# An mLSTM cell with a SwiGLU layer behind it: VectorE's weighing, a scaling step, two loads and a few clears change places

## The chip, the cores and the metric

One core of one Trainium2 chip runs the whole program. The metric is the device time of one execution in microseconds, as the median of several runs. The profile of a run is that of one execution.

## The reference

```python
def _attn_ref(q, k, v, i_gate, f_gate, o_gate):      # q, k, v, o_gate: (4, 8, 768, 40); gates: (4, 8, 768)
    ...                                              # C, n start at 0, m at -1e30
    for t in range(S):
        kt, vt, qt = (k[:, :, t], v[:, :, t], q[:, :, t])
        m_new = np.maximum(f_gate[:, :, t] + m, i_gate[:, :, t])
        f_stab = np.exp(f_gate[:, :, t] + m - m_new)
        i_stab = np.exp(i_gate[:, :, t] - m_new)
        m = m_new
        C = f_stab[:, :, None, None] * C + i_stab[:, :, None, None] * np.einsum('bhd,bhe->bhde', vt, kt)
        n = f_stab[:, :, None] * n + i_stab[:, :, None] * kt
        h_tilde = np.einsum('bhde,bhe->bhd', C, qt)
        nq = np.einsum('bhd,bhd->bh', n, qt)[:, :, None]
        denom = np.maximum(np.abs(nq), 1.0)
        o = 1.0 / (1.0 + np.exp(-o_gate[:, :, t]))
        y[:, :, t] = o * h_tilde / denom
    return y

def _moe_ref(x, w_gate, w_val, w_out):               # x: (3072, 320), weights: (320, 1536) twice, (1536, 320)
    g = x @ w_gate
    silu = g * (1.0 / (1.0 + np.exp(-g)))
    val = x @ w_val
    return silu * val @ w_out
```

The cell's output, with its heads side by side, is the input x of the layer. The three weight matrices come as float64, the rest as float32.

## The kernel before

**Tiling.** The 768 tokens of the sequence are cut into six groups of 128. Group 0 is attended in one piece (128 tokens at once), the later ones in halves of 64 with a state C carried between them. The 32 pairs of batch and head are worked in two parts P of 16. For each group of 4 x 128 tokens the layer then computes 12 blocks of 128 hidden features (`NFC`), and their product with `w_out`.

**Order.** The order on every engine is the order of the program's text: there is no planner, each engine has one queue, and an instruction that waits holds back all behind it. DMAs are issued from SP's queue, some from GpSimd's (the value halves of the weights). Two pools of PSUM banks, "cell" and "gen", have four banks each and hand them out in turn.

**The head (0 to 27 us of the profile).** SP issues the loads of q, k, v and the output gate for group 0, then the first weights. VectorE, GpSimd and ScalarE clear paddings and build masks; PE computes group 0's decay weights as sums in PSUM (`first_mask` L569, `first_inputs` L573, `first_maxima` L578), ScalarE exponentiates them, PE transposes q and k (`turn_one`, L352, which reads the padded columns too), computes scores (`first_scores`), the output rows (`first_own`), their transposes (`seam`, L508) and the first state (`first_state` L640, two banks of "gen"). `first_kept` (L643) copies that state to SBUF on ScalarE. `spread` copies the densely loaded q and k into tiles of 64 columns a head of which 40 are filled; `q_sb` and `k_sb` have their 24 columns of padding cleared. `keep1` is a row of ones with a zero at the head of every 64, needed by `late_sums`. `late_gates` (L156) loads the gates of groups 1 to 5, 80 KB each, which `late_sums` reads in the hidden layer of group 0.

**The weights.** They arrive as pairs of 32-bit words in pieces (`piece_load`: a gate half from SP's queue and a value half in two parts from GpSimd's). Pieces 0 to 3 hold one block each, pieces 4 to 7 two. Pieces 2 and 3 land in a part of `h_sb`, and their loads wait for a small memset there (L693, L701). A block is converted to float32 in three steps (`convert`): `scale` on ScalarE (two instructions, L226 into `top` and L228 into `low`; `top` has one buffer, `low` two), `join` on VectorE (L235, L236) and `rounded` (L243), on GpSimd by default and on VectorE where `on_vector` or the call says so. Block 0 is done in two portions (L253, L254). Silu's function table is loaded ahead of time by a one-element activation on `warm` (L715).

`fill("add", 12, False)` (L557) issues 12 matmuls on zeros into a spare part of a bank, whose result nobody reads.

**Group 0's hidden layer (27 to 88 us).** The loop at L1060 calls `hidden(0, m, ...)` for the 12 blocks: 20 matmuls into two banks of "gen" (L759), then the steps handed over as `first` (conversions of later blocks), then Silu on ScalarE (L764) and the product on VectorE (L765). Behind each block the steps of `slots[m]` follow: the attention of group 1 is spread over them. `do_scores` puts group 1's scores into all four banks of "cell"; `do_weigh` (`weigh`, L392) multiplies them with the decay weights on VectorE; `do_add` takes banks of "cell" again; `do_intra` reads the weighed scores.

```python
for m in range(NFC):
    first = [run(convert, j, V if j in on_vector else None) for j in ahead[m]]
    first += {10: [run(scale, 12), run(join, 12)], 11: [run(convert, 13)]}.get(m, [])
    hidden(0, m, first, amid.get(m, ()))
    for f in slots.get(m, ()):
        f()
```

Groups 1 to 5 follow with fewer products a block (`gated` L929, `project_seven` L830, L835). The change does not touch them.

Of the kernel before, what the change touches and what calls it, by code (L numbers as in the profile page):

```python
# [24 lines left out]
def kernel(  # L25
# [18 lines left out]
    nc = tc.nc  # L44
    B, H, S, D = q.shape
# [28 lines left out]
    def flat(t):  # L74
        return t.rearrange("p c t -> p (c t)")
# [22 lines left out]
    def half(i):  # L98
        return slice(i * SUB, (i + 1) * SUB)
# [5 lines left out]
    def heads(P):  # L105
        return slice(P * UH, (P + 1) * UH)

    k_sb = const.tile([128, BH, DP], F32)
    q_sb = const.tile([128, BH, DP], F32)
    v_sb = const.tile([128, BH, D1], F32)  # L110
    o_sb = const.tile([128, BH, D], F32)
# [19 lines left out]
    f_sb, i_sb, keep1 = (x_flat[0:BH, ds(5 * L + n * (NS - 2) * SUB, (NS - 2) * SUB)].rearrange("p (s t) -> p s t", t=SUB)  # L131
                         for n in range(3))
# [8 lines left out]
    def copy(eng, dst, src):  # L141
        if eng is nc.scalar:
            nc.scalar.copy(dst, src)
        else:
            eng.tensor_copy(dst, src)

    def gate_rows(a):
        return a.rearrange("b h s -> (b h) s")
# [7 lines left out]
    def late_gates():  # L156
        nc.sync.dma_start(out=flat(f_sb), in_=gate_rows(f_gate)[:, L:])
        nc.sync.dma_start(out=flat(i_sb), in_=gate_rows(i_gate)[:, L:])
# [7 lines left out]
    def piece_load(p, home=None, parts=(0, 1, 2)):  # L166
        kind, m, n = PIECES[p]
        if kind == "gv":
            a, d = NKC, n * 128
            gate_w, val_w = (w[:, m * 128:(m + n) * 128].rearrange("(c p) f -> p c f", p=HP) for w in (moe_w_gate, moe_w_val))  # L170
            src = [(slice(0, HP), slice(0, NKC), gate_w), (slice(HP, 128), slice(0, NKC - 1), val_w[:, 1:]),
                   (slice(HP, 128), slice(NKC - 1, NKC), val_w[:, 0:1])]
        else:
            a, d = n, DM
            src = [(slice(0, 128), slice(0, n), moe_w_out[m * 128:(m + n) * 128].rearrange("(a p) d -> p a d", p=128))]
        if src[0][2].dtype == F32:
            for r, cs, w in [src[x] for x in parts if x < len(src)]:
                if kind == "o":
                    nc.sync.dma_start(out=wo_sb[r, m:m + n, :], in_=w)
                else:  # L180
                    for x in range(n):
                        nc.sync.dma_start(out=wgv_sb[r, m + x, cs], in_=w[:, :, ts(x, 128)])
            return
        if p in homes:
            raw = homes[p]
        else:
            if p < 4:
                if p == 0:
                    homes["raw"] = conv.tile([128, 4 * NKC * 128], U32, name="raw")
                base = homes["raw"] if p < 2 else raw_h.rearrange("p m t -> p (m t)").bitcast(U32)  # L190
                raw = base[:, ds(2 * (p % 2) * a * d, 2 * a * d)]
            elif home is None:
                raw = conv.tile([128, 4 * NKC * 128], U32, name="raw")
            else:
                raw = home.rearrange("p a t -> p (a t)").bitcast(U32)
            raw = homes[p] = raw[:, 0:2 * a * d]
        for x in parts:
            if x < len(src):
                r, cs, w = src[x]
                eng = nc.gpsimd if x else nc.sync  # L200
                eng.dma_start(out=raw[r].rearrange("p (a d) -> p a d", a=a)[:, cs], in_=w.bitcast(U32))
        words = raw.rearrange("p (a d two) -> p a d two", two=2, a=a)
        raws[p] = (words[:, :, :, 0], words[:, :, :, 1])
        split(p)
# [4 lines left out]
    def split(p):  # L209
        if p in raws:  # L210
            lo, hi = raws.pop(p)
            kind, m, n = PIECES[p]
            if kind == "gv":
                for c in range(n):
                    r = slice(c * 128, (c + 1) * 128)
                    blocks[m + c] = (lo[:, :, r], hi[:, :, r], wgv_sb[:, m + c])
            else:
                for c in range(0, n, 2):
                    blocks[NFC + (m + c) // 2] = (lo[:, c:c + 2], hi[:, c:c + 2], wo_sb[:, m + c:m + c + 2, :])

    def scale(j):
        if j in blocks:
            lo, hi, dst = blocks[j]
            a, d = hi.shape[1], hi.shape[2]
            top = conv.tile([128, NKC * 128], F32, name="top", bufs=1).rearrange("p (a d) -> p a d", a=a)
            nc.scalar.mul(top, hi.bitcast(F32), 2.0 ** -112)  # L226
            low = conv.tile([128, NKC * 128], I32, name="low").rearrange("p (a d) -> p a d", a=a)
            nc.scalar.mul(low, lo, 2.0 ** -29)  # L228
            blocks[j] = (low, top.bitcast(U32), dst)

    def join(j):
        if j in blocks:
            lo, top, dst = blocks[j]
            both = dst.bitcast(U32)
            nc.vector.tensor_scalar(both, top, scalar1=3, scalar2=None, op0=ALU.logical_shift_left)  # L235
            nc.vector.scalar_tensor_tensor(both, in0=top, scalar=0x80000000, in1=both, op0=ALU.bitwise_and,  # L236
                                           op1=ALU.bitwise_or)
            blocks[j] = (lo, dst.bitcast(I32))

    def rounded(j, eng=None):  # L240
        if j in blocks:
            lo, dst = blocks.pop(j)
            (eng or nc.gpsimd).tensor_tensor(dst, dst, lo, op=ALU.add)  # L243
# [13 lines left out]
    def convert(j, eng=None):  # L257
        scale(j)
        join(j)
        rounded(j, eng)  # L260
# [6 lines left out]
    def spread(eng, x, dst, P):  # L267
        copy(eng, dst[:, heads(P), 0:D], dense[:, x])
# [16 lines left out]
    nc.gpsimd.affine_select(mask, mask, compare_op=ALU.is_ge, fill=NEG, base=0, pattern=[[1, L]], channel_multiplier=-1)  # L285
    nc.vector.memset(keep0, 1.0)
    nc.vector.memset(step0, 0.0)
    nc.gpsimd.memset(q_sb[:, :, D:], 0.0)
    nc.gpsimd.memset(v_sb[:, :, D:], 1.0)
    ident_b = early.tile([128, 128], BF16)  # L290
    nc.vector.tensor_copy(ident_b, ident)
# [259 lines left out]
    def fill(name, n, thin):  # L551
        for x in range(n):
            i = x % 2
            if thin:
                nc.tensor.matmul(spare_of[name, 1][half(i)], lhsT=junk[:, 0:SUB], rhs=junk[:, H * D1:], start=True, stop=True)
            else:
                nc.tensor.matmul(spare_of[name, i], lhsT=junk[half(i), 0:128], rhs=junk[half(i), H * D1:], start=True,  # L557
                                 stop=True)
# [4 lines left out]
    A, V, G = nc.scalar, nc.vector, nc.gpsimd  # L563
# [17 lines left out]
    def first_exp(P):  # L581
        for x in range(B):
            h = P * UH + x * HH
            nc.scalar.activation(W0[:, h:h + HH], wps[P, x], AF.Exp)
# [6 lines left out]
    def first_values(P):  # L591
        nc.gpsimd.tensor_tensor(vw_sb[:, heads(P)], v_sb[:, heads(P)], w_end[:, heads(P)].to_broadcast([128, UH, D1]),
                                op=ALU.mult)
# [49 lines left out]
    def first_kept(P, ps, eng):  # L643
        copy(eng, state(2)[:, P * UA:(P + 1) * UA], ps)
# [11 lines left out]
        first_inputs(1, x)  # L656
    spread(V, 0, q_sb, 0)
    spread(G, 1, k_sb, 0)
    nc.vector.memset(k_sb[:, :, D:], 0.0)
    nc.vector.memset(keep1, 1.0)  # L660
    nc.vector.memset(keep1[:, :, 0:1], 0.0)
    first_exp(0)
    turn_one(0, q_sb, qT, (V, A))
    turn_one(0, k_sb, kT, (V, A))
# [16 lines left out]
    turn_one(1, k_sb, kT, (A, A), "gen")  # L681
    nc.scalar.activation(warm, warm, AF.Sigmoid)
    first_values(1)
    late_gates()
    first_x(0)
    first_own(1)
    first_x(1)
# [11 lines left out]
    first_gate(1, (G, V), V)  # L699
    piece_load(2)  # L700
    nc.gpsimd.memset(flat(raw_h)[:, 2 * NKC * 128:2 * NKC * 128 + 1], 0.0)  # L701
    piece_load(3)
    piece_load(4)
    portion(0, slice(0, 2))
# [6 lines left out]
    blocks.pop(0, None)  # L711
    join((0, 2))
    rounded((0, 2), V)
    fill("add", 12, False)
    nc.scalar.activation(warm, warm, AF.Silu)  # L715
    convert(1, V)
    first_kept(0, ps0, A)
    first_kept(1, ps1, A)
    convert(2, V)
# [314 lines left out]
    def load_all(dst, a, n, eng=nc.sync):  # L1034
        for P in range(2):
            load(dst, a, n, P, eng)

    run = lambda f, *a, **b: (lambda: f(*a, **b))


    on_vector = (9, 10, 11)
    ahead = {0: [], 1: [3], 2: [4], 3: [5], 4: [6], 5: [7], 6: [8], 7: [9], 8: [10], 9: [11], 10: [], 11: []}
    slots = {
        0: [run(piece_load, 5), run(piece_load, 6, wo_sb)],
        1: [run(late_sums)],
# [4 lines left out]
        6: [run(piece_load, 7, parts=VALUE)] + [run(turn_one, P, k_sb, kT, (A, A)) for P in range(2)] + [run(weights_cap, 0), run(weights_cap, 1), run(piece_load, 8)],  # L1050
        7: [run(weights_sub, 1, 0), run(weights_sub, 1, 1), run(weights_exp, 0), run(weights_exp, 1), run(weigh_values, G, 0),
            run(weigh_values, G, 1)],
        8: [run(nc.gpsimd.memset, q_sb, 0.0), run(do_scores), run(piece_load, 9), run(load_all, o_sb, o_gate, 1)],
        9: [run(do_weigh, 0), run(do_weigh, 1), run(do_decayed, 2)],
        10: [run(do_add, 1, (0,)), run(rounded, 12), run(load_squares, q_sq, q, 2, (0,))],
        11: [run(do_intra, 0), run(do_inter, 1, 0), run(do_gather, 1, 0, False), run(piece_load, 10),
             run(load_squares, q_sq, q, 2, (1,))],
# [1 line left out]
    amid = {8: [run(turn_one, P, q_sb, qT, (A, A)) for P in range(2)], 11: [run(do_add, 1, (1,)), run(do_state, 2)]}  # L1059
    for m in range(NFC):  # L1060
        first = [run(convert, j, V if j in on_vector else None) for j in ahead[m]]
        first += {10: [run(scale, 12), run(join, 12)], 11: [run(convert, 13)]}.get(m, [])
        hidden(0, m, first, amid.get(m, ()))
        for f in slots.get(m, ()):
            f()
# [115 lines left out]
```

## Time and profile before

| what | value |
|---|---|
| median of 3 runs | 507.34 us (507.01 to 509.08) |
| profiled execution | 507.06 us, span 505.3 us |
| granted TensorE clock | 0.999 |
| PE busy in 0:26.99 | 24.62 us |
| PE busy in 26.99:31.84 | 4.56 us of 4.85 |
| PE busy in 31.84:53.50 | all 21.66 us |
| PE busy in 70:96 | 25.87 us of 26.00 |
| DMA in 26.99:31.84 | 233 GB/s, share of the engines 1.06 |

The span runs from the first to the last instruction on the core; the time of the execution has 1.76 us more around it. Busy time of an engine leaves out instructions that only wait, branch or issue DMAs. The share of DMA can come out above 1, since a packet's time holds its own waiting.

### The profile page before, as it was taken

What the parts mean: (1) busy time and instruction counts of PE and PEld (TensorE: products, weight loads), DVE (VectorE), ACT (ScalarE), POOL (GpSimd) and SP (SyncE); (2) the same over time, 40 slices, a digit from 0 to 9 for tenths busy, and PEclk for the clock granted to TensorE, in tenths of its full rate; (3) what the DMA queues carried; (4) which work ended last, traced back from release to release, by engine and by line L of the source; (5) the groups of instructions that cost most, each with busy time, mean ns of one, the idle gap of its engine ahead of it and who ended that gap; (6) DMA issues with size and microseconds to landing.
All of it is one profiled execution on the core that took longest, in us unless ns stands there. A gap on an engine that the chain in (4) does not pass through costs nothing.

```text
span 505.3 us, 15069 instructions
## 1 busy us (share of the span) xinstructions
PE 499.4 (99%) x6427; PEld 423.6 (84%) x6427; DVE 334.6 (66%) x544; ACT 209.3 (41%) x407; POOL 260.2 (51%) x292
## 2 busy tenths in 40 slices
PE   8999999999999999999999999999999999999997
PEld 3855555767888899988899888899888899988897
DVE  6779767889998687578376677477568554233421
ACT  3775783467262256323248312339321340223210
POOL 3743533458877834466633357643357650166710
PEclk9999999999999999999999999999999999999999
DMA  9999998797706991403992502991101200000001
GB/s 143 188 262 220 170 229 180 155 173 106 104 4 100 161 93 48 54 3 58 165 111 34 87 4 44 165 131 20 42 3 22 34 2 27 27 0 1 1 14 39
DMA packets 184746, 43.29 MB, mean 86 GB/s; under 512 B 173000, under 2 KB 180184, under 8 KB 184040
## 3 DMA queue, kind: packets, MB, share of 16 engines
q1 hardware_dynamic: 183284, 38.26, 47.6%
q0 software_dynamic: 1264, 4.02, 3.1%
q8 instruction: 50, 0.82, 0.7%
q14 instruction: 16, 0.13, 0.1%
q10 hardware_dynamic: 132, 0.07, 0.0%
HBM read 35.68 MB, written 4.01 MB: 79 GB/s over the span
## 4 chain that ended last, share of the span: by engine, by line
PE 92%; SPq 3%; DMA 2%; DVE 2%; issue 1%; ACT 1%; DVEq 0%; ACTq 0%
PE gv_x L929 26%; PE o_ps L830 21%; PE gv_y L929 21%; PE gv_ps L759 9%; PE o_ps L776 5%; PE inter L434 2%; PE sp L385 2%; PE intra L443 2%; SPq L139 2%; DMA raw<-in_moe_w_gate_dram 2%; PE add L411 2%; PE o_ps L835 1%; SPq L265 1%; DVE w_sb L520 0%; DVE wgv_sb L236 0%
## 5 line engine op out<-in xcount | busy, mean ns | idle before, releaser
L929 PE MATMUL gv_x<-xT,wgv_sb 64*128 64x256 f32 x720 | 89.1, 377 | 0.0
L929 PEld LDWEIGHTS gv_x<-xT,wgv_sb 64*128 64x128 f32 x720 | 69.5, 187 | 7.9 <-issue 0.2
L830 PE MATMUL o_ps<-wo_sb,h_sb 128*128 128x160 f32 x456 | 63.9, 300 | 0.0
L830 PEld LDWEIGHTS o_ps<-wo_sb,h_sb 128*128 128x128 f32 x456 | 62.3, 190 | 1.7 <-issue 1.7
L977 ACT ACTIVATE h_sb<-gv_x 128x256 f32<-128x256 f32 x30 | 11.5, 384 | 116.3 <-PE gv_x L929 116.3
L759 PE MATMUL gv_ps<-xT,wgv_sb 64*128 64x512 f32 x240 | 53.6, 595 | 0.6 <-DVE wgv_sb L243 0.6
L759 PEld LDWEIGHTS gv_ps<-xT,wgv_sb 64*128 64x128 f32 x240 | 24.3, 187 | 24.8 <-issue 23.2
L929 PE MATMUL gv_y<-xT,wgv_sb 64*128 64x256 f32 x360 | 43.9, 376 | 0.0
L929 PE MATMUL gv_y<-q_sb,wgv_sb 64*128 64x256 f32 x360 | 43.9, 376 | 0.0
L396 POOL TENSOR_TENSOR vw_sb<-v_sb,w_sb 128x656 f32<-128x656 f32 x10 | 13.6, 1361 | 49.0 <-ACT w_sb L535 38.1
L929 PEld LDWEIGHTS gv_y<-q_sb,wgv_sb 64*128 64x128 f32 x360 | 35.0, 187 | 3.9
L929 PEld LDWEIGHTS gv_y<-xT,wgv_sb 64*128 64x128 f32 x360 | 35.0, 187 | 3.9
L535 ACT ACTIVATE w_sb<-w_sb,g_T 128x64 f32<-128x64 f32 x128 | 31.0, 333 | 0.0
L929 PE MATMUL gv_x<-q_sb,sw 64*128 64x256 f32 x240 | 30.9, 376 | 0.0
L830 PE MATMUL o_ps<-wT,S 128*128 128x160 f32 x216 | 30.2, 299 | 0.0
L830 PEld LDWEIGHTS o_ps<-wT,S 128*128 128x128 f32 x216 | 29.6, 190 | 0.0
L970 POOL TENSOR_TENSOR tmp<-tmp 128x512 f32<-128x512 f32 x15 | 20.0, 1333 | 16.8 <-DVE tmp L969 16.8
L950 POOL TENSOR_TENSOR h_sb<-x_sb 128x512 f32<-128x512 f32 x12 | 15.7, 1305 | 24.6 <-ACT x_sb L949 24.6
L950 POOL TENSOR_TENSOR h_sb<-tmp 128x512 f32<-128x512 f32 x13 | 16.5, 1271 | 21.5 <-ACT tmp L949 21.5
L797 POOL TENSOR_TENSOR S<-h_sb 128x256 f32<-128x256 f32 x30 | 22.6, 755 | 9.2 <-DVE h_sb L950 7.2
L776 PE MATMUL o_ps<-wo_sb,h_sb 128*128 128x320 f32 x96 | 27.4, 439 | 0.0
L969 DVE TENSOR_TENSOR tmp<-tmp,gv_y 128x1024 f32<-128x1024 f32 x15 | 18.1, 1205 | 13.7 <-PE gv_y L929 12.0
(234 smaller groups left out, 1008.2 us busy)
## 6 DMA issues: line engine op xcount, KB each, us to landing
w_sb<-M_dram SPq DMA_DIRECT2D x10, 512.0 KB, 6.7
v_sb<-in_v_dram SPq DMA_DIRECT2D x12, 320.0 KB, 6.2
o_sb<-in_o_gate_dram SPq DMA_DIRECT2D x12, 320.0 KB, 5.8
raw<-in_moe_w_out_dram SPq DMA_DIRECT2D x3, 1280.0 KB, 7.1
k_sb<-in_k_dram SPq DMA_DIRECT2D x10, 320.0 KB, 7.2
x_sq<-k_sb SPq DMA_DIRECT2D x64, 40.0 KB, 3.3
q_sb<-in_q_dram SPq DMA_DIRECT2D x32, 64.0 KB, 3.6
raw<-in_moe_w_gate_dram SPq DMA_DIRECT2D x3, 640.0 KB
```

The source lines that it names most:

```text
L139: eng.dma_start(out=dst[:, heads(P), 0:D], in_=tokens(a, c, P))
L396: eng.tensor_tensor(vw_sb[:, heads(P)], v_sb[:, heads(P)], w_sb[:, heads(P), last].to_broadcast([128, UH, D1]), op=ALU.mult)
L535: nc.scalar.activation(w_sb[:, h], w_sb[:, h], AF.Exp, bias=g_T[:, n, h:h + 1], scale=-1.0)
L759: nc.tensor.matmul(ps[i], lhsT=wgv_sb[half(i), m, kc, :], rhs=x[half(i), kc, :], start=(kc == 0), stop=(kc == NKC - 1))
L776: nc.tensor.matmul(ps[u], lhsT=hid(g, m)[:, ts(u, L)], rhs=wo_sb[:, m, :], start=(m == 0), stop=(m == NFC - 1))
L797: eng.tensor_tensor(S1[:, k], lo[:, second_half], hi[:, second_half], op=ALU.add)
L830: nc.tensor.matmul(node[x][:, i], lhsT=lhs(k)[:, ts(i, L)], rhs=rhs(k), start=start and k == 0 and i == 0, stop=stop and k == KH - 1, skip ...
L929: nc.tensor.matmul(ps[:, i, cols], lhsT=lhs(c)[half(i)], rhs=rhs(c)[half(i)], start=start and c == 0, stop=stop and c == n - 1, skip_group ...
L950: (nc.vector if k == KH - 1 else nc.gpsimd).tensor_tensor(h_sb[:, 2 * k + 1], uw[:, 0], uw[:, 1], op=ALU.mult)
L969: nc.vector.tensor_tensor(uw, uw, y, op=ALU.add)
L970: nc.gpsimd.tensor_tensor(uw[:, :, second_half], uw[:, :, second_half], uw[:, :, first_half], op=ALU.add)
L977: nc.scalar.activation(h[:, first_half], x[:, 0, first_half], AF.Silu)
```

## The change

In the head, `q_sb`'s padding is cleared by VectorE behind its copy of q instead of by GpSimd at the start, and `keep1` is built by GpSimd behind its copy of k instead of by VectorE. The two late gate loads move in SP's queue from ahead of piece 2's gate half to behind it. Six of the 12 matmuls on zeros go. Block 1's two scaling instructions stand ahead of Silu's table load on ScalarE instead of behind it.

In group 0's hidden layer, block 11 is no longer converted in one go behind block 9's matmuls. Its scaling stays there; its join and rounding (still on VectorE) move to the slot behind block 9, thus behind block 9's product. The weighing of group 1's scores moves from the slot behind block 9 into the slot behind block 8, so that on VectorE it stands ahead of block 9's product and block 11's join. ScalarE's order is the same there, as is PE's and GpSimd's.

```diff
@@ -285,7 +285,6 @@
-    nc.gpsimd.memset(q_sb[:, :, D:], 0.0)
@@ -656,9 +655,10 @@
     spread(V, 0, q_sb, 0)
     spread(G, 1, k_sb, 0)
+    nc.vector.memset(q_sb[:, :, D:], 0.0)
     nc.vector.memset(k_sb[:, :, D:], 0.0)
-    nc.vector.memset(keep1, 1.0)
-    nc.vector.memset(keep1[:, :, 0:1], 0.0)
+    nc.gpsimd.memset(keep1, 1.0)
+    nc.gpsimd.memset(keep1[:, :, 0:1], 0.0)
     first_exp(0)
@@ -681,7 +681,6 @@
     first_values(1)
-    late_gates()
     first_x(0)
@@ -699,6 +698,7 @@
     piece_load(2)
     nc.gpsimd.memset(flat(raw_h)[:, 2 * NKC * 128:2 * NKC * 128 + 1], 0.0)
+    late_gates()
     piece_load(3)
     piece_load(4)
@@ -711,9 +711,9 @@
     rounded((0, 2), V)
-    fill("add", 12, False)
+    fill("add", 6, False)
+    convert(1, V)
     nc.scalar.activation(warm, warm, AF.Silu)
-    convert(1, V)
     first_kept(0, ps0, A)
     first_kept(1, ps1, A)
     convert(2, V)
@@ -1038,8 +1038,8 @@
-    on_vector = (9, 10, 11)
-    ahead = {0: [], 1: [3], 2: [4], 3: [5], 4: [6], 5: [7], 6: [8], 7: [9], 8: [10], 9: [11], 10: [], 11: []}
+    on_vector = (9, 10)
+    ahead = {0: [], 1: [3], 2: [4], 3: [5], 4: [6], 5: [7], 6: [8], 7: [9], 8: [10], 9: [], 10: [], 11: []}
@@ -1050,8 +1050,9 @@
-        8: [run(nc.gpsimd.memset, q_sb, 0.0), run(do_scores), run(piece_load, 9), run(load_all, o_sb, o_gate, 1)],
-        9: [run(do_weigh, 0), run(do_weigh, 1), run(do_decayed, 2)],
+        8: [run(nc.gpsimd.memset, q_sb, 0.0), run(do_scores), run(piece_load, 9), run(load_all, o_sb, o_gate, 1),
+            run(do_weigh, 0), run(do_weigh, 1)],
+        9: [run(join, 11), run(rounded, 11, V), run(do_decayed, 2)],
@@ -1059,7 +1060,7 @@
-        first += {10: [run(scale, 12), run(join, 12)], 11: [run(convert, 13)]}.get(m, [])
+        first += {9: [run(scale, 11)], 10: [run(scale, 12), run(join, 12)], 11: [run(convert, 13)]}.get(m, [])
```

## The prediction, made before the changed kernel ran

> **What bounds the kernel.** I read the page first, then the timeline of each engine for the first 32 us and for 58 to 90 us (the two stretches that the diff touches), the landing times of single DMAs there, and last the sums by window.
>
> The page:
>
> ```profile
> span 505.3 us, 15069 instructions
> PE 499.4 (99%) x6427; PEld 423.6 (84%) x6427; DVE 334.6 (66%) x544; ACT 209.3 (41%) x407; POOL 260.2 (51%) x292
> ```
>
> PE is busy for all but 5.9 us. About 1.2 us of that lies before its first matmul and 3.1 us behind its last. What ordering can still win is thus some 1.6 us of holes and PE work that need not be there. PE's timeline around the start of the hidden layer (start, us, engine, line, operation, the idle time before it and its releaser):
>
> ```profile
> 25.99 0.65 PE L557 MATMUL add<-junk 64*128 64x184 bf16 x12
> 26.99 4.56 PE L759 MATMUL gv_ps<-xT,wgv_sb 64*128 64x512 f32 x20 [0.35 <-DVE wgv_sb L243]
> 31.84 21.73 PE L759 MATMUL gv_ps<-xT,wgv_sb 64*128 64x512 f32 x100 [0.29 <-DVE wgv_sb L243]
> ```
>
> The twelve idle matmuls end 0.35 us before block 0's weights are ready; block 0 ends ahead of block 1's weights. Five blocks in 21.73 us are 4.35 us a block, so block 1 could start at 26.99 + 4.35 = 31.34; it starts at 31.84. The hole is worth 0.50 us, of which 0.29 shows as idle (ends of matmuls are modelled). From 31.84 on, the trace gives PE only one more hole, 0.13 us at 70.2. Now ScalarE in the same stretch:
>
> ```profile
> 26.59 0.58 ACT L254 ACTIVATE low<-raw 128x384 int32<-128x384 uint32 x1
> 27.18 1.28 ACT L715 ACT_TABLE_LOAD   x1
> 28.48 0.20 ACT L715 ACTIVATE warm<-warm 128x1 f32<-128x1 f32 x1
> 28.59 0.76 ACT L226 ACTIVATE top<-raw 128x640 f32<-128x640 f32 x1
> 29.25 0.77 ACT L228 ACTIVATE low<-raw 128x640 int32<-128x640 uint32 x1
> 29.93 0.76 ACT L143 COPY C<-add 128x328 f32<-128x328 f32 x2
> ```
>
> Block 1's scaling (L226, L228) stands behind Silu's table; the two copies of the first state (L143) stand behind the scaling. And the DMA that brings the last part of piece 1, issued at 22.01 (the DMA view of that moment, columns: size, us to landing):
>
> ```profile
> raw<-in_moe_w_val_dram POOLq DMA_DIRECT2D x1, 64.0 KB, 6.0
> ```
>
> It lands at 28.0. So the table load is not what it seems: for 0.8 of its 1.28 us the scaling had no data anyway.
>
> **Block 1's scaling ahead of the table (the core).** Call T the start of L226. Of block 2 the last value part was issued at 24.23 and took 7.3 us, landing at 31.53, and its L226 starts at 31.70: 0.17 from landing to start. With the landing unchanged T becomes 28.0 + 0.17 = 28.17 instead of 28.59, 0.42 earlier. VectorE's three steps follow from T as they do now (L243 ends at 31.70 = T + 3.11, PE starts at T + 3.25), so the weights admit block 1 at 31.42.
>
> But the change adds a wait in ScalarE's queue: L226 now waits for the DMA with the table, the warm-up and the two copies of the state queued behind it. Who waits for those: PE. Block 1's two accumulators take the banks of the two first-state products (the banks rotate by four; both first matmuls of that block wait for ScalarE). By the rows: L228 ends at T + 1.44, the table takes 1.28, the first copy starts 0.11 behind the warm-up's start, and the pair of copies takes 0.76: they end at T + 1.46 + 1.28 + 0.02 + 0.11 + 0.76 = T + 3.63. With 0.07 for the release (0.04 from ScalarE's exp to PE at 9.4, 0.13 from L243 to PE at 31.7), PE's second bank is free at T + 3.70. That is later than the weights. So block 1 starts at the later of 31.34 and T + 3.70. At T = 28.17 that is 31.87: nothing gained, one wait traded for another. The whole 0.50 needs T at 27.64, a landing at 27.47.
>
> **Late gates behind block 2.** The two gate loads (80 KB each; 1.01 and 0.42 us of issue on SP) leave the place before piece 2's gate half. SP issues them between 23.28 and 24.90, where it now waits for a 0.12 us memset of GpSimd (L701) before piece 3: 1.43 fits into 1.62. If not, piece 3's gate half is late by tenths; cover is 1 us, since its value half lands later than it. VectorE reads the gates at 37.64, eight us behind their landing. What it does to T: 160 KB at the 233 GB/s of the window 26.99:31.84 are 0.7 us of traffic that no longer lie beside piece 1's value half, but piece 2's gate half (320 KB, issued at 22.68 in both kernels) moves up into their place. Bounds for the landing: 0 to 0.7 us earlier. A later one has no cause in the bytes, but has one in who shares the engines (second rival). I take 0.2, near the low end, since the queue never runs empty.
>
> **q's padding to VectorE, keep1 to GpSimd.** VectorE's cast of the mask (L293) takes 0.82 us beside GpSimd's 0.74 us memset of q's padding; the cast of the same shape before it (L291) takes 0.23. Without it the mask is ready some 0.5 us earlier and PE's eight mask matmuls start when the three before them end, about 0.25 earlier than 2.73. VectorE gets 0.70 (the padding, priced by k's, L659) for 0.59 and 0.07 (keep1): 0.04 us more, at 7.7 to 9.1, ahead of k's transposes at 9.97. GpSimd's keep1 costs 0.62 (as L328) at 8.8, in a hole that lasts to 10.42. The 0.25 then runs down the PE-paced head to the Sigmoid and GpSimd's gating, and piece 1's value half is issued up to 0.25 earlier. It does not move block 0: its first scaling (L253 at 24.69) waits for piece 0's gate half, issued at 16.42 and 8.2 us under way, in a stretch where the DMA share is above 1. Bounds: 0 to 0.25 on T, taken 0.15.
>
> **Six idle matmuls fewer.** 6 x 0.054 = 0.32 us less PE work, worth nothing: PE then waits 0.67 instead of 0.35 for L243. Of the clock, the window view grants 1.00 through the present gap and 0.91 for 502.5:505.2; at half rate that is 0.5 us, so the drop comes 2.5 us behind the last matmul. 0.67 is far from it.
>
> **Weighing ahead of block 11's joining.** The same instructions in another order on VectorE, behind block 8's product:
>
> ```profile
> 75.25 0.68 DVE L765 TENSOR_TENSOR h_sb<-tmp,gv_ps 128x512 f32<-128x512 f32 x1
> 75.84 0.64 DVE L235 TENSOR_SCALAR wgv_sb<-top 128x640 uint32<-128x640 uint32 x1
> 76.52 1.24 DVE L236 SCALAR_TENSOR_TENSOR wgv_sb<-top,wgv_sb 128x640 uint32<-128x640 uint32 x1
> 77.89 0.83 DVE L243 CUSTOM_DVE_ANT_0 wgv_sb<-wgv_sb,low 128x1280 uint16<-128x1280 uint16 x1
> 78.64 0.68 DVE L765 TENSOR_TENSOR h_sb<-tmp,gv_ps 128x512 f32<-128x512 f32 x1
> 79.23 2.48 DVE L392 TENSOR_TENSOR w_sb<-sp,w_sb 128x512 f32<-128x512 f32 x4
> ```
>
> New order: weighing 75.84 to 78.32, block 9's product to 78.92, then block 11's join and rounding at the undisturbed 0.48 + 0.83 + 0.83 plus gaps of 0.2: ready at about 81.15. PE reaches block 11 at 82.13. Cover 1.0 us, 0.5 if PE is 0.5 earlier. Join 11 frees the scaling buffer for block 12 at 80.2, so ScalarE's Silu of block 10 slips by about 0.5, but VectorE's product that needs it stands behind block 12's join and ends at 83.0 against 83.57. Nothing of PE waited for the weighing (intra starts at 87.89). Sum: 0, bounds 0 and +0.33: at the prices beside GpSimd's work (0.66, 1.81, 0.83, block 10's) the weights come at 82.46.
>
> **The sum.** T = 28.17 - 0.2 - 0.15 = 27.82; block 1 starts at 31.52 instead of 31.84: -0.32 us. Next late would be block 2's banks, freed by block 0's product (35.43, plus 0.14) against 35.9: just free. The profiled execution took 507.06 (span 505.3, 1.76 around it), near the median 507.34; 0.32 off it gives 506.74, and off the median 507.0.
>
> **A rule against it.** Behind the table load at 27.18 the next instruction starts 0.02 after its end; at 110.80 likewise (1.28, next at 112.09). The Trainium skill (ScalarE: Activation LUTs, What ACT_TABLE_LOAD costs) has each switch at about 1283 ns plus a drain of about 1380 ns. The load agrees with 1.28; the drain shows behind neither, and with it the sum would be +1.06 instead of -0.32, about 508.4.
>
> **Rivals.**
> 1. No gain, 507.3: the value half lands at 28.0 as before and the bank wait replaces the weight wait at 31.87. For it: piece 2 fills the gap that the gates leave. Against: two shifts, both towards earlier.
> 2. Slower: the landing comes later and, with the table now in series behind it, delays the copies and PE one for one. It decides from a landing at 27.97. Price: parts of piece 2 took 7.3 us where those of piece 1 took 6.0; at 7.3 the landing is 29.3, block 1 starts at 33.17, +1.33, 508.7; at half of that 508.0. For it: the old order hid the table in the DMA's time. Against: no bytes are added.
> 3. Block 11 late: the present gain less 0.33, 507.3.
> 4. The head's 0.25 reaches block 0 too and the hole closes: -0.75, 506.6. Against: the landing at 24.6.
> 5. A drain behind the table: its place is ahead of the copies, its price bounded by the rows at 0.02. The page's figure gives 508.4.
>
> **Numbers.** Forecast 0.5; no gain or block 11 late 0.25; slower by the landing 0.08; head 0.07; drain 0.02; 0.08 for stalls or shifts of traffic that no row shows. A measurement of this kernel tells 0.5% (2.5 us) from no change, and every case named lies inside it; of the 0.08, 0.03 falls beyond on the fast side and 0.05 on the slow one. The range runs from rival 4 less what the runs scatter below their median (0.33) to the half price of rival 2 with a little of the same: 506.2 to 508.2.
>
> **What would show it.** Right: L226 starts before 28 ahead of the table, block 1 starts near 31.5 and the row of idle before it is below 0.2. If ScalarE's copies are named as its releaser, rival 1 or 2. Wrong in the middle: idle time of PE between 81 and 83 with L243 as releaser. Wrong altogether: a granted clock below 1.00 before 500 us, or any hole of PE above 1 us.

## The result, and the profile after

The changed kernel takes 507.25 us (median of 22 runs, 506.54 to 509.01); the kernel before, run between them on the same chip, 508.67 us (22 runs, 507.01 to 509.69). The ratio of the means is 0.9976, with a 95% interval of 0.9968 to 0.9984: about 1.2 us less (1.42 between the medians). The time lies in the forecast range of 506.2 to 508.2 and near its 507.0, but 0.32 us had been expected, not 1.2, and from another place.

One number matters for all that follows. The profiled execution of before that the prediction was worked from took 507.06 us. That is 1.6 us below the median of the 22 runs: it was an uncommonly quick execution. The profiled execution of after took 507.54, near its median. Set side by side the two profiles thus show no gain at all. The page of after:

```profile
span 505.7 us, 15057 instructions
PE 499.6 (99%) x6421; PEld 426.9 (84%) x6421; DVE 335.3 (66%) x543; ACT 208.8 (41%) x407; POOL 261.4 (52%) x293
```

Line numbers of after are one lower than those of before as far as L658 (the weighing is L391, the add products of the second state L410); Silu's table is one higher (L716), and the lines of the hidden layer are the same.

**The head of the hidden layer.** ScalarE and then PE from 26 us on (start, us, engine, line, operation, idle before it and its releaser):

```profile
26.39 0.55 ACT L254 ACTIVATE low<-raw 128x384 int32<-128x384 uint32 x1
27.69 0.80 ACT L226 ACTIVATE top<-raw 128x640 f32<-128x640 f32 x1 [0.75 <-DVE wgv_sb L236]
28.39 0.80 ACT L228 ACTIVATE low<-raw 128x640 int32<-128x640 uint32 x1
29.21 1.28 ACT L716 ACT_TABLE_LOAD   x1
30.50 0.20 ACT L716 ACTIVATE warm<-warm 128x1 f32<-128x1 f32 x1
30.61 0.75 ACT L143 COPY C<-add 128x328 f32<-128x328 f32 x2
```

```profile
26.89 19.32 PE L759 MATMUL gv_ps<-xT,wgv_sb 64*128 64x512 f32 x86 [0.87 <-DVE wgv_sb L243]
```

The scaling now starts at 27.69, ahead of the table, 0.90 earlier than before. PE's row of the hidden layer no longer breaks behind block 0: it runs from 26.89 through all 86 matmuls up to 46 us. Block 1 starts at 31.25 instead of 31.84, 0.59 earlier.

**Where that was given back.** Blocks 2 and 3 follow every 4.3 us, block 4 comes 4.80 behind block 3 and block 5 4.55 behind block 4. By block 5 after is at 49.19, before was at 49.08. The waits from 38 to 46 us (engine, what it waited with and for; total, times, longest):

```profile
ACT top L226 <- DMA raw<-in_moe_w_gate_dram: 4.1, 1, 4.1
...
PEld gv_ps L759 <- POOL wgv_sb L243: 0.9, 1, 0.9
```

ScalarE stands for 4.1 us before piece 4's gate half, which SP issued at 25.00 and which landed at 40.62; in before's first profile it had landed at 39.18. GpSimd's rounding of block 4 starts 0.96 later than in before (43.04 against 42.08), and the weight loads of PE wait for it.

**The weighing.** VectorE and PE from 75 to 86 us:

```profile
76.15 0.67 DVE L765 TENSOR_TENSOR h_sb<-tmp,gv_ps 128x512 f32<-128x512 f32 x1
76.75 2.47 DVE L391 TENSOR_TENSOR w_sb<-sp,w_sb 128x512 f32<-128x512 f32 x4
79.14 0.67 DVE L765 TENSOR_TENSOR h_sb<-tmp,gv_ps 128x512 f32<-128x512 f32 x1
79.74 0.48 DVE L235 TENSOR_SCALAR wgv_sb<-top 128x640 uint32<-128x640 uint32 x1
80.25 0.82 DVE L236 SCALAR_TENSOR_TENSOR wgv_sb<-top,wgv_sb 128x640 uint32<-128x640 uint32 x1
81.11 0.82 DVE L243 CUSTOM_DVE_ANT_0 wgv_sb<-wgv_sb,low 128x1280 uint16<-128x1280 uint16 x1
```

```profile
81.37 1.14 PE L410 MATMUL add<-vw_sb,k_sb 64*64 64x41 f32 x64
82.44 2.85 PE L759 MATMUL gv_ps<-xT,wgv_sb 64*128 64x512 f32 x12
```

The order is the one foretold, with the undisturbed prices for block 11 (0.48, 0.82, 0.82). Its weights are ready at 81.93, PE takes them at 82.44 without a wait.

### The profile page after: what moved, and what is told of

Read it like the earlier page. It is cut to its first block, busy times and chain, and to the rows that moved or that the text cites. A ratio compares the mean times of both kernels' runs of the same rounds, so it can differ in the third digit from the quotient of the medians.

```text
span 505.7 us, 15057 instructions
## 1 busy us (share of the span) xinstructions
PE 499.6 (99%) x6421; PEld 426.9 (84%) x6421; DVE 335.3 (66%) x543; ACT 208.8 (41%) x407; POOL 261.4 (52%) x293
## 4 chain that ended last, share of the span: by engine, by line
PE 85%; DMA 4%; SPq 4%; DVE 2%; POOL 2%; ACT 2%; issue 1%; POOLq 0%; ACTq 0%; DVEq 0%
PE gv_x L929 26%; PE o_ps L830 21%; PE gv_y L929 21%; PE gv_ps L759 4%; SPq L368 3%; DMA raw<-in_moe_w_gate_dram 3%; PE sp L384 2%; PE o_ps L776 2%; PE inter L433 2%; PE intra L442 1%; DMA w_sb<-M_dram 1%; PE o_ps L835 1%; PE add L410 1%; PE wps L568 1%; PE tp_kq L351 1%
## 5 line engine op out<-in xcount | busy, mean ns | idle before, releaser
L759 PEld LDWEIGHTS gv_ps<-xT,wgv_sb 64*128 64x128 f32 x240 | 28.7, 187 | 21.4 <-issue 14.4
L929 PE MATMUL gv_y<-q_sb,sw 64*128 64x256 f32 x200 | 27.0, 388 | 0.0
```

The lines of the kernel that those rows point to most:

```text
L759: nc.tensor.matmul(ps[i], lhsT=wgv_sb[half(i), m, kc, :], rhs=x[half(i), kc, :], start=(kc == 0), stop=(kc == NKC - 1))
L929: nc.tensor.matmul(ps[:, i, cols], lhsT=lhs(c)[half(i)], rhs=rhs(c)[half(i)], start=start and c == 0, stop=stop and c == n - 1, skip_group ...
```

## The experiments

All ratios are to the kernel before, run in turn with each kernel on its chip. "Stall" means PE's idle time at the add products of the second state.

**1. The kernel before once more.** No edit; which of the two profiles is typical?

> The kernel before, unchanged, for a second profile of it. Over 22 runs its median is 508.67 us, 1.6 above its profiled run of 507.06; the changed kernel's median is 507.25. Theory D (delivery): in a typical run of the kernel before, the gate half of piece 4 lands later than the 39.2 us of the first profile (in the profile of the changed kernel it lands at 40.6 and PE stands still for half a microsecond ahead of block 4). Then this profile, if its time is near 508.7, shows a landing near 41.5 to 42.5, an idle PE of 0.5 to 1.2 us ahead of block 4 or 5, released by GpSimd's rounding, and the hole of 0.3 ahead of block 1 as in the first profile. Rival H: the extra time lies elsewhere (in the head ahead of block 0, in the tail behind PE's last matmul, or outside the span); then block 4 starts within 13.0 us of block 1 as in the first profile (44.8 against 31.8).

Measured: 509.37 us, ratio 1.0006 (0.9987 to 1.0025). Its profiled execution took 509.40, 0.5 above the median of 508.9 that before has over 35 runs on that chip. It has the trouble in another place than was expected; block 4 comes 12.95 behind block 1, three ordinary blocks. First, rows of the profile that the prediction was worked from, PE and then GpSimd:

```profile
81.05 1.14 PE L411 MATMUL add<-vw_sb,k_sb 64*64 64x41 f32 x64
```

```profile
70.88 2.81 POOL L396 TENSOR_TENSOR vw_sb<-v_sb,w_sb 128x656 f32<-128x656 f32 x2 [10.18 <-ACT qT L143]
73.63 1.81 POOL L1038 MEMSET q_sb<- 128x2048 f32 x1
```

And the repeat: PE, then VectorE, then GpSimd from 72 to 86 us:

```profile
72.56 8.85 PE L759 MATMUL gv_ps<-xT,wgv_sb 64*128 64x512 f32 x40
82.48 0.28 PE L411 MATMUL add<-vw_sb,k_sb 64*64 64x41 f32 x2 [1.06 <-DVE w_sb L392]
83.08 1.14 PE L411 MATMUL add<-vw_sb,k_sb 64*64 64x41 f32 x62 [0.32 <-DVE w_sb L392]
```

```profile
75.27 0.67 DVE L765 TENSOR_TENSOR h_sb<-tmp,gv_ps 128x512 f32<-128x512 f32 x1
75.86 2.73 DVE L235 TENSOR_SCALAR wgv_sb<-top 128x640 uint32<-128x640 uint32 x1
78.63 1.23 DVE L236 SCALAR_TENSOR_TENSOR wgv_sb<-top,wgv_sb 128x640 uint32<-128x640 uint32 x1
80.00 1.14 DVE L243 CUSTOM_DVE_ANT_0 wgv_sb<-wgv_sb,low 128x1280 uint16<-128x1280 uint16 x1
...
81.66 2.47 DVE L392 TENSOR_TENSOR w_sb<-sp,w_sb 128x512 f32<-128x512 f32 x4
```

```profile
73.00 3.51 POOL L396 TENSOR_TENSOR vw_sb<-v_sb,w_sb 128x656 f32<-128x656 f32 x2 [12.16 <-ACT low L228]
76.45 1.80 POOL L1038 MEMSET q_sb<- 128x2048 f32 x1
78.21 2.25 POOL L420 TENSOR_TENSOR C<-C,dec 128x328 f32<-128x328 f32 x2
```

Read from the bottom. GpSimd begins its product of v and the weights at 73.00; in the prediction's profile it began at 70.88. So VectorE's shift for block 11 (L235), which started behind the clear of `q_sb` before, now starts beside the last 0.64 us of the product and has the whole 1.80 us of the clear beside it. It takes 2.73 instead of 0.64 and ends 0.34 behind the clear. The weighing starts at 81.66 instead of 79.23. It reads the scores out of the four banks of "cell", and the add products need these banks: PE starts the first of them 0.2 behind the end of the weighing's first instruction, and the next 0.2 behind the second (2.47 / 4 = 0.62 each: 82.28 and 82.90). PE stands for 1.06 + 0.32 = 1.38 us. By the starts of its blocks it loses a little more: from block 9 to block 11 it takes 11.58 us here, 9.86 in the first profile of before and 9.99 in after.

**2 to 4. Three parts alone, each on the kernel before.** The scaling ahead of the table; the gates behind block 2; the clears.

```diff
@@ b_scale
-    nc.scalar.activation(warm, warm, AF.Silu)
     convert(1, V)
+    nc.scalar.activation(warm, warm, AF.Silu)
@@ b_gates
     first_values(1)
-    late_gates()
...
+    late_gates()
     piece_load(3)
@@ b_pads
-    nc.gpsimd.memset(q_sb[:, :, D:], 0.0)
...
+    nc.vector.memset(q_sb[:, :, D:], 0.0)
     nc.vector.memset(k_sb[:, :, D:], 0.0)
-    nc.vector.memset(keep1, 1.0)
-    nc.vector.memset(keep1[:, :, 0:1], 0.0)
+    nc.gpsimd.memset(keep1, 1.0)
+    nc.gpsimd.memset(keep1[:, :, 0:1], 0.0)
```

> The kernel before with one part alone: block 1's scaling ahead of Silu's table. Prediction's step: T goes from 28.6 to about 28.2, the two state copies end at T + 3.6, and PE starts block 1 at T + 3.7 = 31.9: no gain at the start of block 1, with ScalarE's copy named as releaser instead of L243; time within 0.3 us of the kernel before. Rival: the copies do not hold PE back (a different bank), then block 1 starts near 31.4, 0.4 earlier. Theory D on the total: scaling alone does not hasten the DMAs of piece 4 except through piece 5's loads, so the total moves by 0 to -0.4.

> The kernel before with one part alone: the late gate loads behind piece 2's gate half. Prediction's step: piece 1's value half lands 0 to 0.7 us earlier than 28.0 (0.2 taken); as the scaling still stands behind the table, block 1 still starts at 31.8. Total: 0, at most 0.1 either way. Theory D: piece 4's gate half has the same bytes ahead of it, so nothing in its landing either: 0. If the late gates are what delays it, the total falls by 0.5 or more.

> The kernel before with one part alone: q's padding cleared by VectorE, keep1 by GpSimd. Prediction's step: the mask's cast shrinks from 0.82 to about 0.25 us, the PE-paced head runs 0.25 to 0.4 us earlier, piece 1's value half is issued as much earlier; block 0 still starts at 26.9 to 27.0 (piece 0's landing), block 1 still near 31.8 (table). Total by the prediction: 0 to -0.1. Theory D: SP issues pieces 2 to 4 as much earlier too, and if block 4 is late by delivery, the total falls by 0.3 to 0.5.

Measured: 508.94 us and 1.0003 (0.9984 to 1.0022); 509.13 and 0.9999 (0.9982 to 1.0017); 508.69 and 0.9994 (0.9974 to 1.0014). None of the three shows a gain, though the intervals would allow one of 0.8, 0.9 and 1.3 us. The stall stands in the first and the third at 1.08 + 0.32. In the second it is absent: its block 0 started at 27.91, 0.9 later than in before, its block 9 1.6 later, and the shift began behind the clear instead of beside it.

The third profile shows that such a stall can cost more than itself:

```profile
83.13 1.14 PE L410 MATMUL add<-vw_sb,k_sb 64*64 64x41 f32 x62 [0.32 <-DVE w_sb L391]
84.19 4.54 PE L759 MATMUL gv_ps<-xT,wgv_sb 64*128 64x512 f32 x12
```

From 84.56 to 87.97 the granted clock is 0.50, and these 12 matmuls take 4.54 us instead of the 2.85 of after; the execution took 510.93, the slowest of its twelve. The stalls of the repeat and of the scaling alone are as long, and their clock stays at 1.00.

The scaling alone shows what the prediction called the first rival. ScalarE and PE of that kernel:

```profile
28.41 0.78 ACT L226 ACTIVATE top<-raw 128x640 f32<-128x640 f32 x1 [1.20 <-DMA raw<-in_moe_w_val_dram]
...
31.31 0.75 ACT L143 COPY C<-add 128x328 f32<-128x328 f32 x2
```

```profile
27.06 4.56 PE L759 MATMUL gv_ps<-xT,wgv_sb 64*128 64x512 f32 x20 [0.74 <-DVE wgv_sb L243]
...
31.78 4.55 PE L759 MATMUL gv_ps<-xT,wgv_sb 64*128 64x512 f32 x19 [0.15 <-ACT C L143]
```

ScalarE waits for piece 1's value half (landed 28.23), and PE's block 1 for the copies of the state behind the table. The bank that ends the wait is that of the first copy: block 1 starts 31.78 - 28.41 = 3.37 behind the scaling, where the prediction had 3.70 by the second one. In the clears alone the mask's cast takes 0.23 instead of 0.82 and PE's mask matmuls start at 2.45 instead of 2.73, as worked out.

**5. The weighing's order alone.**

```diff
-    on_vector = (9, 10, 11)
+    on_vector = (9, 10)
-    ahead = {..., 9: [11], 10: [], 11: []}
+    ahead = {..., 9: [], 10: [], 11: []}
-        8: [..., run(load_all, o_sb, o_gate, 1)],
-        9: [run(do_weigh, 0), run(do_weigh, 1), run(do_decayed, 2)],
+        8: [..., run(load_all, o_sb, o_gate, 1), run(do_weigh, 0), run(do_weigh, 1)],
+        9: [run(join, 11), run(rounded, 11, V), run(do_decayed, 2)],
...
-        first += {10: [run(scale, 12), ...
+        first += {9: [run(scale, 11)], 10: [run(scale, 12), ...
```

> The kernel before with one part alone: the weighing ahead of block 11's join. The second profile of the kernel before (span 507.6) holds PE for 1.06 + 0.32 us ahead of the first add product, released by the weighing (L392, ending 84.1 instead of 81.7 in the first profile), because VectorE's join of block 11 took 2.73 + 1.23 + 1.14 us beside GpSimd's work instead of 0.48 + 0.83 + 0.83. Theory W: this part alone takes that stall away; time 1.2 to 1.6 us below the kernel before (ratio 0.997 to 0.9975), PE idle 0 at the add products (81 to 83). Rival D (the gain of the whole change comes from the head and from earlier DMAs): within 0.3 us of before, and the stall reappears at block 11's matmuls, released by L243, 1 us or more.

Measured: 507.9 us, 0.9981 (0.9963 to 0.9999), about 1.0 us less. GpSimd's product starts at 71.93 here, the weighing ends at 78.92, and PE has no stall. (The profiled execution took 506.91, 1.0 below its median; a slower one with the new order stands under 8.)

**6. The changed kernel with the weighing put back.** The same lines in reverse.

> The changed kernel with the weighing and block 11's conversion put back as before; the head's four parts stay. Theory W: the stall of 1.0 to 1.4 us at the add products is back, and the head's gain at block 1 (0.3 to 0.6) is spent by block 4 or 5 waiting for piece 4; the time is that of the kernel before within 0.4 us (ratio 0.9992 to 1.0). Rival D: most of the gain stays, ratio 0.998 or less.

Measured: 509.09 us, 1.0015 (0.9988 to 1.0042). The interval lies wholly above that of the changed kernel (0.9968 to 0.9984). PE from 79 us on:

```profile
81.85 0.28 PE L410 MATMUL add<-vw_sb,k_sb 64*64 64x41 f32 x2
82.44 1.14 PE L410 MATMUL add<-vw_sb,k_sb 64*64 64x41 f32 x62 [0.32 <-DVE w_sb L391]
```

A stall of 0.09 + 0.32 is back (the 0.09 is too small to be printed in the row). In this execution the shift lay beside the clear for a part only (0.89), so its stall is 0.4 and not 1.4; the runs' loss is larger than that. Three of its twelve runs had a mean granted clock of 0.996 or 0.997, about what one stretch at half clock as above gives; of the changed kernel's 22 runs none had.

**7. The kernel before without GpSimd's clear of `q_sb`.** If the clear makes the join slow, leaving it out must free the weighing without any change of order. It leaves the padding of q for the later groups uncleared.

```diff
-        8: [run(nc.gpsimd.memset, q_sb, 0.0), run(do_scores), ...
+        8: [run(do_scores), ...
```

> The kernel before without GpSimd's clear of q_sb behind block 8 (1.8 us of GpSimd; the columns beyond the 40 of a head then keep what was there). Theory W, its mechanism: VectorE's join of block 11 (L235, 2.73 us in the second profile, ending 0.3 us behind that clear) is held up by GpSimd's work in the same stretch. Without the clear L235 takes below 1.2 us, the weighing ends 1.3 to 2 us earlier and PE's stall at the add products shrinks from 1.4 to below 0.3 us: 1.0 to 1.4 us faster. Rival: the join waits for something else (its scaling, or block 9's end), or GpSimd's next step (the decay of the state, L420) holds it as long; then L235 ends within 0.5 us of 78.6 and the time is as before.

Measured: 508.34 us, 0.9990 (0.9975 to 1.0006). VectorE and GpSimd:

```profile
77.24 0.48 DVE L235 TENSOR_SCALAR wgv_sb<-top 128x640 uint32<-128x640 uint32 x1
...
80.06 2.48 DVE L392 TENSOR_TENSOR w_sb<-sp,w_sb 128x512 f32<-128x512 f32 x4
```

```profile
71.95 2.81 POOL L396 TENSOR_TENSOR vw_sb<-v_sb,w_sb 128x656 f32<-128x656 f32 x2 [10.84 <-PE sp L385]
74.72 2.59 POOL L420 TENSOR_TENSOR C<-C,dec 128x328 f32<-128x328 f32 x2
```

The shift is back at 0.48, the weighing at 80.06, and PE has no stall. From block 1 to PE's last matmul this execution takes 471.34 us, the repeat of before 472.58: 1.24 less, inside the 1.0 to 1.4 expected. Over the runs that was missed: the medians differ by 0.35, with an interval from a gain of 1.3 to a loss of 0.3. So the trace bears the mechanism out, while its price is not settled by this kernel. GpSimd's product also started 1.05 earlier here, which by itself helps.

**8. The changed kernel once more.**

> The changed kernel, unchanged, on the chip of the three below, for a second profile of it. Theory W (the gain is the stall at the add products that the weighing order removes) and theory P (what the head wins at block 1 is given back at blocks 4 and 5, where piece 4's gate half lands at 40 to 41): ratio to before 0.997 to 0.9985; block 1 starts at 31.2 to 31.5, block 4 at 44.4 to 45.0, no idle time of PE at the add products (81 to 83). Rival: the stall at blocks 4 and 5 was one run's accident; then block 4 starts within 13.0 us of block 1.

Measured: 507.99 us, 0.9982 (0.9971 to 0.9993). GpSimd's product starts as late as 73.33, and yet there is no stall: the weighing lies beside the clear (76.84 to 78.64) and ends at 78.72, and the shift takes 0.48:

```profile
76.25 2.47 DVE L391 TENSOR_TENSOR w_sb<-sp,w_sb 128x512 f32<-128x512 f32 x4
78.65 0.67 DVE L765 TENSOR_TENSOR h_sb<-tmp,gv_ps 128x512 f32<-128x512 f32 x1
79.24 0.48 DVE L235 TENSOR_SCALAR wgv_sb<-top 128x640 uint32<-128x640 uint32 x1
```

Block 4 again waits for GpSimd's rounding, and starts 4.94 behind block 3, with piece 4's gate half landing at 41.10.

**9 and 10. The head's gain without the scaling, and without the gates.** The changed kernel with one part undone each: the table ahead of the scaling again; the gates ahead of piece 2 again.

> The changed kernel with block 1's scaling behind Silu's table again. Prediction's step: block 1 starts at about 31.8 instead of 31.3, a loss of 0.3 to 0.5. Theory P: that loss is repaid at block 4, whose start is set by piece 4's landing: block 4 starts at 44.6 to 44.9 either way and the time is within 0.2 us of the changed kernel. Rival (the head's gain reaches the end): 0.3 to 0.5 slower than the changed kernel.

> The changed kernel with the late gates ahead of piece 2 again. Prediction's step: piece 1's value half lands about 0.2 us later than in the changed kernel (27.5), and with the table behind the scaling the state copies end as much later: block 1 starts at 31.4 to 31.6 with ScalarE's copy as releaser. Theory P: given back at block 4, total within 0.2 us of the changed kernel. Rival: the late gates' place moves piece 4's landing by 0.5 us or more, and the total with it.

Measured: 507.84 us and 0.9977 (0.9966 to 0.9987); 508.03 us and 0.9984 (0.9970 to 0.9998). Undoing the scaling costs nothing that the runs show (0.9982 for the changed kernel on the same chip). Block 1 starts at 32.25 in that profile, 1.0 later than in after, but 0.65 of that stands at block 0 already; it follows block 0 after 4.71 instead of 4.36. Block 4 starts at 45.44, not at the 44.6 to 44.9 that had been expected. With the gates back the scaling starts at 27.95 and PE waits for the copies:

```profile
26.48 4.56 PE L759 MATMUL gv_ps<-xT,wgv_sb 64*128 64x512 f32 x20 [0.23 <-DVE wgv_sb L243]
31.33 1.98 PE L759 MATMUL gv_ps<-xT,wgv_sb 64*128 64x512 f32 x7 [0.29 <-ACT C L143]
```

From scaling to block 1 it is 3.38, as in the scaling alone. Here block 4 follows block 3 after 4.29, without a wait, and block 11 starts at 81.94, 0.50 earlier than in after. That lead is lost as well, at another place: at 112.66 PE has stood 0.77 for GpSimd's rounding of `wo_sb`.

**11 and 12. Two ways to keep the head's gain.** If piece 4 sets block 4, either less traffic beside it or smaller parts should bring it sooner.

```diff
@@ a_five_later
-        0: [run(piece_load, 5), run(piece_load, 6, wo_sb)],
-        1: [run(late_sums)],
+        1: [run(piece_load, 5), run(piece_load, 6, wo_sb), run(late_sums)],
@@ a_split_four (in piece_load)
+        if p == 4:
+            e = 2 * a * 128
+            room = [raw[:, z * e:(z + 1) * e] for z in range(2)]
+            for x in parts:
+                r, cs, w = src[x]
+                for z in range(2):
+                    (nc.gpsimd if x else nc.sync).dma_start(out=room[z][r].rearrange(...)[:, cs],
+                                                            in_=w[:, :, ts(z, 128)].bitcast(U32))
...
```

> The changed kernel with the loads of pieces 5 and 6 issued one block later (slot 1 instead of slot 0, ahead of the late sums). In the profile of the changed kernel PE loses 0.5 us at block 4 and 0.25 at block 5: piece 4's gate half lands at 40.6, beside piece 5's value half (landing 40.3 and 40.8). Theory P: without piece 5's value half beside it, piece 4's gate half lands 1 to 2 us earlier, block 4 starts 4.3 us after block 3, and the time falls by 0.4 to 0.7 us below the changed kernel. Rival: what piece 4 gains, pieces 5 and 6 or the loads of k lose, and PE waits at block 6 or 8 instead; time as the changed kernel or up to 1 us slower.

> The changed kernel with piece 4's loads cut into one set for each of its two blocks (gate and value), block 4's first, each into its own part of the buffer. Theory P: block 4's gate half lands at 37.5 to 39 instead of 40.6, its join follows at once behind the late sums (about 40.7 instead of 41.5), block 4 starts 4.3 us behind block 3 and the idle 0.5 there and 0.25 at block 5 go: 0.4 to 0.7 us below the changed kernel, ratio to before 0.996 to 0.9975. Rival: smaller packets and two more issues on SP and GpSimd delay what is behind them (pieces 5 and 6, the stores and loads of group 1), and PE waits elsewhere; then as the changed kernel or up to 0.5 slower.

Measured: 510.71 us and 1.0047 (1.0022 to 1.0072); 508.39 and 0.9999 (0.9979 to 1.0019). Both repair block 4 (4.29 behind block 3) and lose elsewhere in the profiled execution. With pieces 5 and 6 a slot later, PE's waits from 40 to 130 us are these:

```profile
PE gv_ps L759 <- DVE wgv_sb L243: 2.0, 1, 2.0
PE tp_g L730 <- ACT x_sq L1038: 1.4, 1, 1.4
PE tp_kq L351 <- ACT w_sb L537: 1.0, 1, 1.0
```

Piece 5's value half now lands at 51 us, 10 later than in after, and what is behind it comes late too. With piece 4 split, q of group 1 lands at 69.94, and PE stands for it:

```profile
70.07 0.89 PE L363 MATMUL tp_kq<-x_sq,q_sb 64*128 64x64 f32 x16 [2.91 <-DMA q_sb<-in_q_dram]
```

These two profiles are not typical, though: they took 514.34, the slowest of its twelve, and 510.97, against medians of 510.71 and 508.39. In both the clock stands at 0.50 for 3.41 us behind the long wait (from 81.85 and from 70.42). With the pieces a slot later all twelve runs have a mean clock of 0.996 or 0.997, so such a stretch belongs to its loss. With piece 4 split only three runs have it; the other nine took 507.06 to 509.39, so the wait of 2.91 is not shown to be there in them. The rival written beside the first of the two was thus right in direction, though the loss against the changed kernel is some 3 us and not up to 1, and PE waits at other places. Of the second the runs say only that the median is not below that of the changed kernel. No version that was run is shown to beat the changed kernel.

## Why the prediction was right, and where it was not

**In the range by luck.** The 507.0 was 0.32 off 507.34, the median of three runs. Over 22 runs that median is 508.67, and 0.32 off it is 508.35, outside the range. The measured time came out near the forecast because the base was taken 1.3 us too low and the gain 1.1 too small. The sign is right, but the gain that the runs show is not the one that was foretold. Nor was the measurement as blunt as the prediction had it (2.5 us): the interval of the result is 0.8 us wide.

**Right: the head's mechanism.** The scaling started at 27.69 against 27.82 foretold, the copies ended 3.67 behind it against 3.63, block 1 began at 31.25 against 31.52. Of the 0.27 that block 1 came earlier 0.13 is the scaling's own start. The rest is the one term mis-sized there: the wait for the second bank, T + 3.70, was taken as the start of the block, and it is the first bank that lets PE begin, at T + 3.37 (3.37 in the scaling alone, 3.38 with the gates back). So block 1 simply follows block 0 at 4.36. By that measure the first rival would have stood at 28.17 + 3.37 = 31.54, not 31.87. That landing moves from execution to execution: value halves of piece 1 landed at 27.50, 27.77, 28.23 and 28.54 in four of the profiles.

**Right: the cheap edits.** Mask cast 0.23, mask matmuls at 2.45, and the clock at 1.00 through 0.87 us of idle time before block 0. Nothing drains behind the table: 29.21 + 1.28 is 30.49, and the next instruction starts at 30.50. The 1380 ns that the Trainium skill (ScalarE: Activation LUTs, What ACT_TABLE_LOAD costs) adds do not appear.

**Wrong: "the weighing: sum 0".** This is the term that carries the result. Alone it gains 1.0 us by the means (b_weigh, with an interval that only just excludes zero), put back it loses the whole gain (a_weigh_back), and none of the three parts run alone shows a gain. The stall stands in four of the six profiles with the old order and GpSimd's clear (in a_weigh_back with 0.4 alone), and in none of the five with the new order and piece 4 as it was. (The six idle matmuls were not undone by themselves.) Two things failed in that step. First, the prediction looked for who waits for the weighing and named the products that read the weighed scores, at 87.89. It passed over the add products at 81.05, which wait not for the result but for the banks that the weighing empties. In the profile it worked from, that cover was about 1.0 us for the first instruction (79.23 + 0.62 + 0.2 = 80.05 against 81.05). Second, it took the join's price from one row, 0.64, where the repeat of before, and the two parts alone that show the stall, have 2.73 to 2.74. It did ask what block 11 costs beside GpSimd's work, but only of the new order, where it counts as a loss; of the old order, where it counts as a gain to be had, it did not ask. (Its terms for block 11 add up to 81.26, not 81.15. In after it is 81.93, as the weighing began 0.91 later there; neither reached PE.)

So a cover of 1.0 us in an execution 1.6 us quicker than the median was read as the kernel's. In the repeat the weighing came 81.66 - 79.23 = 2.43 later and PE only 0.29 later at block 9, which takes the cover and 1.1 us more, as PE's row shows.

**Why the new order is safe.** The weighing takes 2.47 or 2.48 us wherever it lies: beside GpSimd's clear and decay step in after, or behind both in the repeat of before. The shift takes 0.48 alone and 2.73 beside the clear. The change puts the step that does not mind beside the clear, and the shift behind it. In the second profile of after GpSimd ran as late as in the repeat of before, and PE had no stall.

The Trainium skill (SBUF — State Buffer, Who interferes with whom) says that VectorE and GpSimd share one pair of ports under an exclusive lock, that a VectorE instruction with at most one SBUF input outside the two-port modes does not touch it, and that `tensor_scalar` can enter such a mode. The rows agree: the weighing reads one input from PSUM and stays at 2.47; the shift is a `tensor_scalar` and ended 0.34 or 0.35 behind the clear in all four profiles where the two met. That the mode was in use was not tried by itself.

**Wrong: "next late would be block 2's banks".** In after it was block 4's weights, through piece 4's gate half (4.1 us of ScalarE waiting) and GpSimd's rounding, and the head's 0.59 was gone by block 5. That undoing the scaling changes nothing in the runs fits this: 0.9977 with the table first, 0.9976 without. It does not prove it, since tenths of a microsecond are at the edge of what these runs tell; block 4 did not start alike with and without the scaling, and with the gates back the lead was lost at 112 us and not at block 4.

**What stays open.** Why GpSimd's product of v begins at 70.88 in the first profile of before and between 71.93 and 73.33 in eleven others. It starts 0.21 to 0.22 behind the landing of v's first load in all of these (70.66 and 72.78 in before and its repeat), so the question is why v lands late. In the repeat each step on the way is later than in the first profile: piece 4's gate half by 1.6 (39.18 to 40.74), the load into `w_sb` issued 0.8 later, v's loads 0.9. That reads as one delay that is handed on by SP's queue, but no run isolates it. Nor do the runs settle why taking the clear away shows 1.24 in the trace and 0.35 in the medians, or why the clock fell behind one stall of 1.40 us and not behind two others.

## What to carry to other kernels

Before working from a profile, set its own time beside several runs: if it is quicker than most of them, the stall that a change removes may be missing from it, and every cover that it shows must be tested at the price that the same instruction has elsewhere in the trace. Ask of a PSUM reader not only who needs its result, but who needs its bank. Where VectorE must share a stretch with GpSimd, put there the steps whose price does not move (here those that read PSUM) and the steps that do behind it; and expect that a gain ahead of a step paced by DMA may be given back at that step. Look at the granted clock of the profile, too, before a wait in it is priced.

## What was not expected of the hardware

- The 128x640 `uint32` shift on VectorE took 0.48 us alone and 2.73 beside a 1.80 us clear on GpSimd: nearly six times the price. That is more than the clear itself, since it also met the end of GpSimd's product ahead of the clear. The price goes with what it meets: 0.64 and 0.63 beside the decay step (before, b_gates), 1.23 and 1.30 beside the product (block 10's shift in b_gates and b_no_qclear). The join's second step (L236) went from 0.83 to 1.23, the rounding (L243) from 0.83 to 1.14.
- It works both ways: GpSimd's decay step took 2.25 us beside VectorE's join in the repeat of before, and 1.43 in after.
- One and the same load of one program lands 1.6 us apart in two executions (piece 4's gate half in before, 39.18 and 40.74). One share of sixteen can set the landing: of piece 0's gate half in before fifteen shares had landed by 23.48 and the last at 24.60, of piece 4's in the repeat fifteen by 39.45 and the last at 40.74. The cause is not shown.
- A wait of PE of 1.40, 2.03 or 2.91 us (b_pads, a_five_later, a_split_four) was followed by 3.41 us at a granted clock of 0.50, which began 1.4, 0.6 and 0.35 us behind the end of the wait.
